# Loading one batch of queries transposed by DMA instead of transposing it on VectorE, in an attention-then-rational-MLP kernel

## The chip, the cores and the metric

The kernel runs on one core of a Trainium2 chip. The time is device microseconds of one execution, from start to end on that core. Three runs of the kernel before took 273.9, 274.3 and 274.56 us; the median is 274.3 us. All instruction times below come from one more execution, which the hardware profiler recorded.

## The reference

Two stages are chained. First an attention with polynomial sketches, for 4 batches, 4 heads, 1,088 positions and head width 32, all float32:

```python
def phi(x):                                  # 32 values -> 64 products
    a = einsum('rd,bhsd->bhsr', S1, x)       # 8 sketch values
    b = einsum('rd,bhsd->bhsr', S2, x)       # 8 sketch values
    return outer product of a and b, flattened
kv  = sum over s of phi(k)[f] * v[d]         # 64 x 32 per batch and head
z   = sum over s of phi(k)
x   = phi(q) @ kv / (phi(q) @ z + 1e-6)
```

The four heads side by side give 4,352 tokens (4 x 1,088) of width 128. Then a two-layer network of hidden width 2,048, with a rational function between the layers:

```python
h = x @ w_in
g = (a0 + a1*h + a2*h^2 + a3*h^3) / (1 + |b0|*|h| + |b1|*h^2 + 1e-6)
out = g @ w_out                              # 4352 x 128
```

## The kernel before

The whole program is written out by hand as one list of steps, `ORDER` (line 21). Each engine executes its own instructions strictly in the order in which that list produces them, so an instruction that waits holds back everything behind it on the same engine. The same holds for the queues on which DMAs are issued: SyncE (SP) issues nearly all of them, ScalarE (ACT) a few, each in its own program order.

**Keys and values.** Batch by batch, `load_k` and `load_v` (lines 116, 126) fetch them on SP's queue. There is one buffer for each (`k_sb`, `v_sb`). VectorE transposes the keys, TensorE makes the sketches, and the 64-value features times the values are summed on TensorE into a small table per batch (`kvz`).

**Queries.** They are worked off in 13 blocks: blocks 0 to 3 are batch 0, 4 to 6 batch 1, 7 to 9 batch 2, 10 to 12 batch 3; a block of batches 1 to 3 has 384, 384 or 320 positions. `load_q` (line 121) fetches a batch on SP's queue into the one buffer `q_sb`; the steps `lq:1`, `lq:2` and `lq:3` place these loads. In `q_sb` a partition holds a head and a group of positions, and VectorE turns 32x32 blocks (line 320, step `qt`) into `qT`, where a partition holds a head and one of the 32 components. Because of this blocking, column j*32+g of `qT` is position g*34+j; the store undoes that. TensorE makes the sketches of a block (line 401, step `qs`).

From block 3 on (class `Spread`) the sketches must be spread over 128 partitions, and this goes through DRAM, in `copies` (step `qc`): ScalarE copies the sketches out of PSUM (line 407), SP issues four small writes to DRAM (line 412), and, when these have landed, three reads that replicate the rows: one into `a_all` (line 415) and two into `b_all` (line 418). Then VectorE multiplies the two (line 424, step `qf`). TensorE multiplies the features with the table (line 360), VectorE divides, TensorE transposes back, and ScalarE writes the tokens into `xT` (line 390).

**Network.** The tokens are cut into 9 tiles (one of 256, eight of 512) and the work into 17 units of 128 x 4,096 values. For each, TensorE makes h (line 446), ScalarE brings it to SBUF as bf16 (line 452), VectorE forms the denominator (lines 475, 481, 486), ScalarE takes ln and exp(-ln) (lines 537, 541), VectorE multiplies (lines 545, 549, 560), and TensorE applies w_out (line 579). Finished tiles are stored by `store` (line 583): VectorE transposes the PSUM tile into `out_sb` (line 588; two buffers, from the pool `mid`), and four or eight DMAs write it out (line 596). The last tile's DMAs alternate between SP's and ACT's queue.

**Completion counters.** The framework attaches one of eight completion counters to every DMA, in turn, on all queues together. In the built program, a DMA whose counter was last used by another DMA waits on its own queue until that other DMA has landed, whether or not they share data.

The program also issues a few matmuls without use at the start (`turn`, line 166).

Of the kernel before, what the change touches and what calls it, by code (L numbers as in the profile page):

```python
# [11 lines left out]
FP = mybir.dt.float32  # L12
BF = mybir.dt.bfloat16
# [9 lines left out]
kf2:0 qc:0 kp0:0 qf:0 ks1:0 qs:1 kc1:0 kf1:0 qc:1 kp1:0 wo:1 qt:3 kp2:0 qf:1 qt:2 qs:3 kk:0 lq:1 wo:4 lv:1 qp:0 wo:0  # L23
qs:2 qd:0 qc:2 qi:0 qx:0 wo:5 qf:2 qb:0 qp:1 qk:0 qc:3 wo:3 h2:0 qd:1 qi:1 qx:1 kt0:1 h3:0 wo:2 e2:0 qt:5 qt:4 qp:2
kt1:1 e3:0 h1:0 pa1:0 u1:0 w1:0 h0:0 y1:0 qd:2 e1:0 qi:2 qx:2 qs:4 e0:0 qb:1 qb:2 qt:6 ks1:1 qk:1 u0:0 qk:2 ln1:0 w0:0
ks0:1 y0:0 h1:1 kc1:1 ex1:0 kf1:1 lk:2 h3:1 lq:2 e1:1 s1:0 kc0:1 h0:1 e3:1 kf0:1 pa0:0 m1:0 h2:1 qf:3 e0:1 x1:0 qp:3
qc:4 e2:1 kt0:2 h0:2 ln0:0 u1:1 kt1:2 h1:2 w1:1 e0:2 ex0:0 y1:1 ks0:2 h2:2 e1:2 s0:0 qd:3 ln0:1 h3:2 qi:3 m0:0 e2:2
lk:3 qx:3 kp1:1 x0:0 e3:2 ex0:1 u1:2 qb:3 lv:2 G0:0 pd0:1 qk:3 w1:2 ln1:1 G1:0 G2:0 qf:4 G3:0 kc0:2 kk:1 y1:2 ex1:1
G4:0 G5:0 kf0:2 qp:4 ln0:2 s0:1 qs:5 G0:1 qd:4 qc:5 qi:4 ex0:2 qt:7 G1:1 qx:4 m0:1 qb:4 ks1:2 qk:4 s1:1 pa1:1 h2:3
s0:2 kc1:2 m1:1 h3:3 e2:3 kf1:2 h1:3 e3:3 st:0 x1:1 ln1:2 qs:7 x0:1 h0:3 e1:3 kt1:3 m0:2 h2:4 e0:3 pd1:2 pa0:2 u1:3  # L30
h3:4 qt:9 w1:3 e2:4 G2:1 ex1:2 x0:2 h0:4 qf:5 e3:4 kp1:2 s1:2 pa0:3 y1:3 h1:4 qc:7 e0:4 m1:2 ln0:3 qp:5 kt0:3 e1:4
G3:1 x1:2 ex0:3 G4:1 m0:3 G5:1 u1:4 ks0:3 qd:5 ln1:3 qi:5 G0:2 w1:4 G1:2 pa1:3 qx:5 G2:2 y1:4 lv:3 qb:5 G3:2 qk:5
ex1:3 h0:5 m1:3 v0:3 kk:2 ln0:4 h2:5 s1:3 e0:5 qs:6 G4:2 qf:7 ex0:4 h1:5 x0:3 qt:8 qc:6 e2:5 s0:4 e1:5 h3:5 pd0:4
pa1:4 m0:4 h1:6 v1:3 e3:5 x0:4 G5:2 ln1:4 u1:5 h3:6 st:2 e1:6 w1:5 qp:7 ex1:4 x1:3 h0:6 e3:6 y1:5 qd:7 pa0:5 lq:3 G0:3
G2:3 qi:7 s1:4 h2:6 e0:6 m0:5 ln0:5 m1:4 qs:8 G3:3 e2:6 qf:6 G5:3 x1:4 ex0:5 G0:4 u1:6 G1:4 qc:8 ln1:5 qp:6 v0:5 qx:7
w1:6 qb:7 qd:6 G2:4 pa0:6 qi:6 G3:4 qx:6 y1:6 qb:6 qk:7 G4:4 qk:6 ex1:5 h3:7 m0:6 pa1:5 G5:4 qt:10 s1:5 h1:7 e3:7 st:4
h2:7 e1:7 m1:5 ln0:6 x0:5 h0:7 e2:7 x1:5 qs:9 e0:7 h3:8 qf:8 ex0:6 u1:7 h1:8 v0:6 qc:9 ln1:6 w1:7 ks1:3 s0:6 e1:8 G0:5
y1:7 kc1:3 qp:8 ex1:6 h2:8 pd1:6 kc0:3 e3:8 s1:6 ln0:7 h0:8 kf0:3 e2:8 m1:6 G2:5 ex0:7 G3:5 x0:6 G4:5 kf1:3 qd:8 e0:8
qs:10 G5:5 ln1:7 qi:8 u1:8 kp1:3 qx:8 pa0:7 w1:8 qb:8 G0:6 qf:9 qk:8 y1:8 qc:10 h3:9 ex1:7 s0:7 h2:9 e3:9 s1:7 ln0:8
h0:9 m0:7 e2:9 x1:6 G2:6 e0:9 h1:10 x0:7 ex0:8 pd1:7 h1:9 m1:7 pa0:8 s0:8 G3:6 e1:9 u1:9 G0:7 qt:11 ln1:8 qp:9 qt:12  # L40
u0:9 m0:8 h3:10 e1:10 w1:9 qd:9 ex1:8 qf:10 h2:10 x0:8 e3:10 G4:6 x1:7 e2:10 h0:10 y1:9 kk:3 pa0:9 w0:9 qp:10 qi:9
y0:9 e0:10 G1:7 qx:9 qd:10 ln0:9 qi:10 s1:8 qb:9 G5:6 u1:10 G2:7 qk:9 ex0:9 G3:7 qx:10 m1:8 qb:10 G4:7 qk:10 ln1:9
pd1:8 qs:11 h1:11 s0:9 qc:11 w1:10 ex1:9 h0:11 m0:9 e1:11 x1:8 G5:7 e0:11 h3:11 y1:10 pa1:9 G0:8 e3:11 s1:9 h2:11
ln0:10 x0:9 h0:12 m1:9 e2:11 pd0:10 ex0:10 h1:12 u1:11 x1:9 G1:8 ln1:10 G2:8 w1:11 G3:8 e0:12 s0:10 G0:9 e1:12 y1:11
G4:8 ex1:10 G5:8 G1:9 m0:10 ln0:11 G2:9 qf:11 h2:12 s1:10 ex0:11 x0:10 h3:12 pa1:10 m1:10 qs:12 G3:9 s0:11 e2:12 G4:9
pd0:11 qc:12 ln1:11 qp:11 m0:11 x1:10 G5:9 e3:12 G0:10 x0:11 qd:11 ex1:11 G1:10 qi:11 u1:12 G2:10 pa1:11 G3:10 qx:11
w1:12 qb:11 G4:10 qk:11 s1:11 pa0:12 h1:13 y1:12 h2:13 e1:13 m1:11 ln0:12 h3:13 st:6 x1:11 ex0:12 G5:10 qf:12 st:10
qp:12 e2:13 s0:12 e3:13 h0:13 st:8 ln1:12 m0:12 h2:14 u1:13 e0:13 x0:12 ex1:12 h3:14 u0:13 w1:13 e2:14 w0:13 G0:11
# [11 lines left out]
SPLIT_A = (0, 9, 13, 16)  # L60
QUARTER = (16,)
LX = 2
WIDE_S = (3, 5)
WIDE_M = (5,)
WIDE_X = (5, 14)
# [3 lines left out]
def kernel(  # L69
# [29 lines left out]
    consts = ctx.enter_context(tc.tile_pool(name="consts", bufs=1))  # L99
    big = ctx.enter_context(tc.tile_pool(name="big", bufs=1))  # L100
# [5 lines left out]
    mid = ctx.enter_context(tc.tile_pool(name="mid", bufs=2))  # L106
# [31 lines left out]
    for i, s_in in enumerate((S1, S2)):  # L138
        t = consts.tile([128, D], FP, name=f"s_raw{i}")
# [4 lines left out]
                      in_=bass.AP(tensor=k.tensor, offset=k.offset, ap=[[S * D // 32, 128], [W, NM], [1, 4 * D]]))  # L144
    nc.scalar.dma_start(out=k0[:, 0:km].rearrange("p (m x) -> p m x", m=NM - 1)[:, :, 4 * D:],
                        in_=k0_src[:, 0:km].rearrange("p (m x) -> p m x", m=NM - 1)[:, :, 4 * D:])
# [13 lines left out]
    w_out_sb_f = mid.tile([128, nf, d_model], FP, name="w_out_sb_f", tag="w", bufs=2)  # L160
    w_out_src = moe_w_out.rearrange("(fo fi) d -> fi fo d", fi=128)

    idle = consts.tile([128, 512], BF, name="idle")
    nc.vector.memset(idle, 0.0)

    def turn(i, cols=512):
        idle_ps = bank()
        for _ in range(TURNS[i]):
            nc.tensor.matmul(idle_ps[:, :cols], lhsT=idle[:, 0:128], rhs=idle[:, :cols], start=True, stop=True)

    mask = consts.tile([128, H], FP, name="mask")
    mask2 = consts.tile([128, 2], FP, name="mask2")
# [19 lines left out]
    for i in range(2):  # L192
        t = consts.tile([128, D], FP, name=f"sT{i}")
# [14 lines left out]
    for i in range(2):  # L208
        t = consts.tile([128, 2, R, R], FP, name=f"SAB{i}")
        s = sT[i][:, None, 0:R, None] if i == 0 else sT[i][:, None, None, 0:R]  # L210
# [10 lines left out]
    def bank():  # L221
        return att.tile([128, 512], FP, name="att_ps")
# [8 lines left out]
    class Keys:  # L231
# [80 lines left out]
    class Queries:  # L312
# [116 lines left out]
    TC = 512  # L429
# [112 lines left out]

    @skip(WIDE_S)
    def d_s(i, h, hh):
        nc.vector.tensor_mul(out=part_of(i, "s", h), in0=hh, in1=part_of(i, "r", h))  # L545
# [37 lines left out]
    def store(i):  # L583
        t0, tl, f0, per = units[i]
        if f0 + per < nf:
            return
        o = mid.tile([128, TC], FP, name="out_sb")
        nc.vector.transpose(out=o[:, :tl], in_=outs[t0][:, :tl])
        c = t0
        while c < t0 + tl:  # L590
            b = c // S
            ce = min(t0 + tl, (b + 1) * S)
            o_b = out[b * S:(b + 1) * S, :].rearrange("(g j) d -> g j d", g=32)
            j0, j1 = (c - b * S) // 32, (ce - b * S) // 32
            for e in range(d_model // 32):
                (nc.scalar if t0 + tl == n_tok and e % 2 else nc.sync).dma_start(
                    out=o_b[:, j0:j1, e * 32:(e + 1) * 32],
                    in_=o[e * 32:(e + 1) * 32, c - t0:ce - t0].rearrange("p (j d) -> p j d", d=32))
            c = ce
# [34 lines left out]
    def fetch_q(b):  # L634
        if b:
            return load_q(b)
        nc.sync.dma_start(out=q0[:, 512:S], in_=q0_src[:, 512:S])
# [71 lines left out]
```

## Time and profile before

| | us |
|---|---|
| median of three runs | 274.3 |
| the profiled execution, whole | 274.34 |
| its span in the trace | 272.6 |
| PE busy | 258.3 |
| DVE (VectorE) busy | 255.9 |
| ACT (ScalarE) busy | 250.0 |
| three transposes of batch 3's queries (line 320, at 116.4 and 152.6 us) | 1.5 |

The time around the span is 274.34 - 272.6 = 1.7 us. PE, DVE, ACT are the compute engines, SP is the engine whose queue issues DMAs; "SPq" in a line is that queue's own record. "L412" is line 412. In the lists of instructions the first number is the start in us from the start of the span, the second the duration in us; consecutive alike instructions are merged, and "x4" says how many. In the lists of waits the three numbers are the total wait in us, how many waits there were, and the longest.

TensorE's granted clock was 0.998 of full speed over the whole span.

### The profile page before, as it was taken

The page shows a single profiled execution, that of the slowest core. Times are in us where ns is not written, and L with a number is a line of the kernel's source. Part 1 is how long each engine was busy: PE and PEld are TensorE (multiplying, and loading weights), DVE is VectorE, ACT ScalarE, POOL GpSimd, SP SyncE. Part 2 cuts the span into 40 slices and gives each one's busy share as a digit, 9 for nine tenths or more (in the row PEclk, how much of TensorE's full clock was granted, in tenths as well). Part 3 has the DMA queues.
Part 4 walks back from the last instruction along what each step waited for, and adds up shares of the span by engine and source line. Part 5 has one row for each costly group of instructions (what it writes and reads, how often), then busy time and mean ns, then how long its engine had stood idle before and what let it go on. Part 6 is the DMA issues. An engine that isn't in the chain of part 4 may idle for free.

```text
span 272.6 us, 3564 instructions
## 1 busy us (share of the span) xinstructions
PE 258.3 (95%) x1318; PEld 135.4 (50%) x1318; DVE 255.9 (94%) x276; ACT 250.0 (92%) x224; POOL 2.9 (1%) x24
## 2 busy tenths in 40 slices
PE   7989999999999899999999999999999999989591
PEld 3778656963564354535454554434544443434230
DVE  2858999999999999999999999999999999999992
ACT  1377999998999999999999999999999999999980
POOL 4000000000000000000000000000000000000000
PEclk9999999999999999999999999999999999999999
DMA  6992607314025062222304000300126100020005
GB/s 166 294 336 80 204 14 173 111 55 95 2 84 129 14 140 77 73 71 39 96 6 117 11 1 6 120 6 0 23 88 96 20 0 0 0 41 1 0 0 77
DMA packets 30465, 19.53 MB, mean 72 GB/s; under 512 B 20337, under 2 KB 26609, under 8 KB 30449
## 3 DMA queue, kind: packets, MB, share of 16 engines
q1 hardware_dynamic: 28416, 18.87, 26.7%
q10 hardware_dynamic: 2032, 0.45, 0.9%
q8 instruction: 10, 0.16, 0.3%
q14 instruction: 7, 0.05, 0.1%
HBM read 16.16 MB, written 3.15 MB: 71 GB/s over the span
## 4 chain that ended last, share of the span: by engine, by line
PE 37%; ACT 28%; DVE 22%; issue 7%; DMA 2%; SPq 1%; DVEq 0%; ACTq 0%
PE h_ps L446 18%; PE att_ps L579 9%; ACT hh L452 8%; ACT ln L537 8%; ACT r L541 7%; ACT p L532 4%; DVE g L549 4%; DVE s L545 4%; DVE w L486 4%; PE att_ps L360 3%; DVE g L560 3%; DVE w L481 2%; DVE u L475 2%; DMA k_sb<-in_k_dram 2%; PE att_ps L297 1%
## 5 line engine op out<-in xcount | busy, mean ns | idle before, releaser
L446 PE MATMUL h_ps<-xT,w_in_sb 128*128 128x512 f32 (+1 forms) x288 | 125.4, 577 | 1.3 <-ACT hh L452 1.1
L446 PEld LDWEIGHTS h_ps<-xT,w_in_sb 128*128 128x128 f32 x288 | 52.2, 190 | 55.9 <-issue 40.5
L452 ACT CAST hh<-h_ps 128x1024 bf16<-128x1024 f32 x68 | 68.3, 1025 | 3.4 <-PE h_ps L446 2.9
L541 ACT ACTIVATE r<-ln 128x2048 bf16<-128x2048 f32 (+1 forms) x35 | 66.0, 1886 | 0.3
L537 ACT ACTIVATE ln<-w 128x2048 f32<-128x2048 bf16 (+1 forms) x35 | 66.0, 1885 | 0.2
L579 PEld LDWEIGHTS <-w_out 128*128 128x128 bf16 x412 | 39.9, 98 | 52.8 <-issue 18.7
L532 ACT ACTIVATE p<-hh,a_sb 128x2048 bf16<-128x2048 bf16 (+1 forms) x23 | 46.7, 2036 | 0.1
L545 DVE TENSOR_TENSOR s<-hh,r 128x2048 bf16<-128x2048 bf16 (+2 forms) x33 | 40.7, 1241 | 0.2
L486 DVE TENSOR_TENSOR w<-w,u 128x4096 bf16<-128x4096 bf16 (+2 forms) x22 | 39.5, 1795 | 0.1
L579 PE MATMUL att_ps<-g,w_out 128*128 128x512 bf16 (+1 forms) x144 | 34.9, 367 | 4.0 <-DVE g L560 3.8
L579 PE MATMUL att_ps<-r,w_out 128*128 128x512 bf16 (+1 forms) x144 | 34.5, 367 | 0.8 <-ACT r L541 0.8
L549 DVE TENSOR_TENSOR g<-hh,s 128x2048 bf16<-128x2048 bf16 (+1 forms) x30 | 35.1, 1172 | 0.0
L560 DVE TENSOR_TENSOR g<-g,p 128x2048 bf16<-128x2048 bf16 (+1 forms) x30 | 34.8, 1173 | 0.0
L579 PE MATMUL att_ps<-s,w_out 128*128 128x512 bf16 (+1 forms) x124 | 30.0, 365 | 0.0
L481 DVE TENSOR_SCALAR w<-u,b_abs 128x4096 bf16<-128x4096 bf16 (+2 forms) x22 | 23.8, 1090 | 0.1
L475 DVE TENSOR_SCALAR u<-hh 128x4096 uint16<-128x4096 uint16 (+2 forms) x22 | 21.3, 970 | 0.6 <-ACT hh L452 0.2
L360 PEld LDWEIGHTS att_ps<-kvz,q_pT 128*128 128x128 f32 x144 | 17.6, 191 | 5.0 <-DVE q_pT L424 1.1
L360 PE MATMUL att_ps<-kvz,q_pT 128*128 128x66 f32 x144 | 17.9, 273 | 0.9 <-DVE q_pT L352 0.5
L297 PEld LDWEIGHTS att_ps<-v_sb,k_p 128*64 128x64 f32 (+1 forms) x288 | 8.8, 138 | 2.6 <-issue 1.8
L527 DVE TENSOR_SCALAR p<-hh,a_sb 128x2048 bf16<-128x2048 bf16 x12 | 9.6, 804 | 0.0
L297 PE MATMUL att_ps<-v_sb,k_p 128*64 128x64 f32 (+1 forms) x288 | 9.5, 224 | 0.0
L424 DVE TENSOR_TENSOR q_pT<-a_all,b_all 128x768 f32<-128x768 f32 (+1 forms) x10 | 8.9, 895 | 0.0
(60 smaller groups left out, 134.9 us busy)
## 6 DMA issues: line engine op xcount, KB each, us to landing
a_all<-sk_d SPq DMA_DIRECT2D x6, 384.0 KB
b_all<-sk_d SPq DMA_DIRECT2D x12, 192.0 KB
v_sb<-in_v_dram SPq DMA_DIRECT2D x12, 144.0 KB
k_sb<-in_k_dram SPq DMA_DIRECT2D x3, 544.0 KB
q_sb<-in_q_dram SPq DMA_DIRECT2D x3, 544.0 KB
a_all<-sk_d SPq DMA_DIRECT2D x4, 320.0 KB
b_all<-sk_d SPq DMA_DIRECT2D x8, 160.0 KB
out_dram<-out_sb SPq DMA_DIRECT2D x18, 64.0 KB
```

Source lines behind the costliest of these rows:

```text
L360: nc.tensor.matmul(self.nd[:, o:o + 2 * KW], lhsT=self.q_p[:, c, x:x + 128], rhs=kvz[self.b % 2][:, c, :], start=True, stop=True)
L446: nc.tensor.matmul(t[:, x * tl:(x + 1) * tl], lhsT=w_in_sb[:, f * 128:(f + 1) * 128], rhs=xT[:, t0:t0 + tl], start=True, stop=True)
L452: nc.scalar.copy(out=live[i]["hh"][:, part * PW:(part + 1) * PW], in_=live[i]["h", part])
L481: nc.vector.tensor_scalar(out=t[:, c], in0=live[i]["u"][:, c], scalar1=ab1, scalar2=ab0, op0=AX.mult, op1=AX.add)
L486: nc.vector.tensor_mul(out=t[:, c], in0=t[:, c], in1=live[i]["u"][:, c])
L532: nc.scalar.activation(out=part_of(i, "p", h), in_=hh, func=ACT.Identity, scale=a3, bias=a2)
L537: nc.scalar.activation(out=t, in_=live[i]["w"][:, span(h)], func=ACT.Ln, bias=1.0 + 1e-6)
L541: nc.scalar.activation(out=part_of(i, "r", h), in_=live[i]["ln"], func=ACT.Exp, scale=-1.0)
L545: nc.vector.tensor_mul(out=part_of(i, "s", h), in0=hh, in1=part_of(i, "r", h))
L549: nc.vector.tensor_mul(out=part_of(i, "g", h), in0=hh, in1=part_of(i, "p" if horner(i, first(h)) else "s", h))
L560: nc.vector.tensor_mul(out=g, in0=g, in1=part_of(i, "s" if horner(i, first(h)) else "p", h))
L579: nc.tensor.matmul(outs[t0][:, :tl], lhsT=w_sb[y][:, f0 + x, :], rhs=part_of(i, key, h)[:, c:c + tl], start=done[0] == 0, stop=done[0] == ...
```

## The change

The queries of batch 3 are no longer loaded into `q_sb` by one DMA on SP's queue (it stood near 101 us). Four DMAs on ACT's queue, one per head, write them into a buffer of their own, `qT_sb`, already transposed: each reads a [1088, 32] matrix of float32 with its axes swapped. In the built program each of the four has 32 x 1,088 = 34,816 runs of one element (4 bytes). The step `lq:3` moves from line 34 of the list to right behind `lq:2`; in ACT's built order the four issues stand behind the first `r` (line 541) and ahead of the next copy of h (line 452). The three transposes of blocks 10 to 12 on VectorE fall away. Since the columns of `qT_sb` are positions in their natural order, the store uses another row order for batch 3.

To make room, the idle matmuls' tile shrinks from 512 to 128 columns (the matmuls read it four times over), and `out_sb` gets one buffer instead of two.

The built program numbers the completion counters 0 to 7. In the changed one the DMAs of this neighbourhood get them so: head 0 of the new load 6, keys of batch 2 counter 7, head 1 counter 0, queries of batch 2 counter 1, heads 2 and 3 counters 2 and 3. Then come the DMAs of block 4 and behind it: the four writes of its sketches 4, 5, 6, 7, its `a_all` 0, its two `b_all` 1 and 2, and the keys of batch 3 counter 3; the values of batch 2 and block 5's DMAs stand behind these on SP's queue.

```diff
 ORDER:  ... lk:2 h3:1 lq:2
+ lq:3
         e1:1 s1:0 kc0:1 ...          (line 26)
...
-pa1:4 m0:4 h1:6 v1:3 e3:5 x0:4 G5:2 ln1:4 u1:5 h3:6 st:2 e1:6 w1:5 qp:7 ex1:4 x1:3 h0:6 e3:6 y1:5 qd:7 pa0:5 lq:3 G0:3
+pa1:4 m0:4 h1:6 v1:3 e3:5 x0:4 G5:2 ln1:4 u1:5 h3:6 st:2 e1:6 w1:5 qp:7 ex1:4 x1:3 h0:6 e3:6 y1:5 qd:7 pa0:5 G0:3 G2:3
...
+NATURAL = (3,)
...
     def load_q(b):
+        if b in NATURAL:
+            t = big.tile([128, S], FP, name="qT_sb")
+            for h in range(H):
+                nc.scalar.dma_start(out=t[h * D:(h + 1) * D, :], in_=q[b, h].rearrange("s d -> d s"))
+            return t
...
-    idle = consts.tile([128, 512], BF, name="idle")
+    idle = consts.tile([128, 128], BF, name="idle")
...
         def transposes(self):
+            if self.b in NATURAL:
+                self.qT = self.q_sb[:, self.c0:self.c0 + self.n]
+                return
...
-        o = mid.tile([128, TC], FP, name="out_sb")
+        o = mid.tile([128, TC], FP, name="out_sb", bufs=1)
...
-            o_b = out[b * S:(b + 1) * S, :].rearrange("(g j) d -> g j d", g=32)
+            o_b = out[b * S:(b + 1) * S, :].rearrange("(j g) d -> g j d" if b in NATURAL else "(g j) d -> g j d", g=32)
```

More of the change, by code (lines that the diff above doesn't have):

```diff
@@ L25 @@
 kt1:1 e3:0 h1:0 pa1:0 u1:0 w1:0 h0:0 y1:0 qd:2 e1:0 qi:2 qx:2 qs:4 e0:0 qb:1 qb:2 qt:6 ks1:1 qk:1 u0:0 qk:2 ln1:0 w0:0
[L26 to L29, printed above, removed]
@@ L30 @@
-s0:2 kc1:2 m1:1 h3:3 e2:3 kf1:2 h1:3 e3:3 st:0 x1:1 ln1:2 qs:7 x0:1 h0:3 e1:3 kt1:3 m0:2 h2:4 e0:3 pd1:2 pa0:2 u1:3
-h3:4 qt:9 w1:3 e2:4 G2:1 ex1:2 x0:2 h0:4 qf:5 e3:4 kp1:2 s1:2 pa0:3 y1:3 h1:4 qc:7 e0:4 m1:2 ln0:3 qp:5 kt0:3 e1:4
-G3:1 x1:2 ex0:3 G4:1 m0:3 G5:1 u1:4 ks0:3 qd:5 ln1:3 qi:5 G0:2 w1:4 G1:2 pa1:3 qx:5 G2:2 y1:4 lv:3 qb:5 G3:2 qk:5
-ex1:3 h0:5 m1:3 v0:3 kk:2 ln0:4 h2:5 s1:3 e0:5 qs:6 G4:2 qf:7 ex0:4 h1:5 x0:3 qt:8 qc:6 e2:5 s0:4 e1:5 h3:5 pd0:4
-pa1:4 m0:4 h1:6 v1:3 e3:5 x0:4 G5:2 ln1:4 u1:5 h3:6 st:2 e1:6 w1:5 qp:7 ex1:4 x1:3 h0:6 e3:6 y1:5 qd:7 pa0:5 lq:3 G0:3
@@ L35 @@
[L35 to L44, printed above, removed]
@@ L45 @@
-G4:8 ex1:10 G5:8 G1:9 m0:10 ln0:11 G2:9 qf:11 h2:12 s1:10 ex0:11 x0:10 h3:12 pa1:10 m1:10 qs:12 G3:9 s0:11 e2:12 G4:9
+ks0:1 y0:0 h1:1 kc1:1 ex1:0 kf1:1 lk:2 h3:1 lq:2 lq:3 e1:1 s1:0 kc0:1 h0:1 e3:1 kf0:1 pa0:0 m1:0 h2:1 qf:3 e0:1 x1:0
+qp:3 qc:4 e2:1 kt0:2 h0:2 ln0:0 u1:1 kt1:2 h1:2 w1:1 e0:2 ex0:0 y1:1 ks0:2 h2:2 e1:2 s0:0 qd:3 ln0:1 h3:2 qi:3 m0:0
+e2:2 lk:3 qx:3 kp1:1 x0:0 e3:2 ex0:1 u1:2 qb:3 lv:2 G0:0 pd0:1 qk:3 w1:2 ln1:1 G1:0 G2:0 qf:4 G3:0 kc0:2 kk:1 y1:2
+ex1:1 G4:0 G5:0 kf0:2 qp:4 ln0:2 s0:1 qs:5 G0:1 qd:4 qc:5 qi:4 ex0:2 qt:7 G1:1 qx:4 m0:1 qb:4 ks1:2 qk:4 s1:1 pa1:1
@@ new lines @@
+h2:3 s0:2 kc1:2 m1:1 h3:3 e2:3 kf1:2 h1:3 e3:3 st:0 x1:1 ln1:2 qs:7 x0:1 h0:3 e1:3 kt1:3 m0:2 h2:4 e0:3 pd1:2 pa0:2
+u1:3 h3:4 qt:9 w1:3 e2:4 G2:1 ex1:2 x0:2 h0:4 qf:5 e3:4 kp1:2 s1:2 pa0:3 y1:3 h1:4 qc:7 e0:4 m1:2 ln0:3 qp:5 kt0:3
+e1:4 G3:1 x1:2 ex0:3 G4:1 m0:3 G5:1 u1:4 ks0:3 qd:5 ln1:3 qi:5 G0:2 w1:4 G1:2 pa1:3 qx:5 G2:2 y1:4 lv:3 qb:5 G3:2 qk:5
+ex1:3 h0:5 m1:3 v0:3 kk:2 ln0:4 h2:5 s1:3 e0:5 qs:6 G4:2 qf:7 ex0:4 h1:5 x0:3 qt:8 qc:6 e2:5 s0:4 e1:5 h3:5 pd0:4
+pa1:4 m0:4 h1:6 v1:3 e3:5 x0:4 G5:2 ln1:4 u1:5 h3:6 st:2 e1:6 w1:5 qp:7 ex1:4 x1:3 h0:6 e3:6 y1:5 qd:7 pa0:5 G0:3 G2:3
@@ new lines @@
+qi:7 s1:4 h2:6 e0:6 m0:5 ln0:5 m1:4 qs:8 G3:3 e2:6 qf:6 G5:3 x1:4 ex0:5 G0:4 u1:6 G1:4 qc:8 ln1:5 qp:6 v0:5 qx:7 w1:6
+qb:7 qd:6 G2:4 pa0:6 qi:6 G3:4 qx:6 y1:6 qb:6 qk:7 G4:4 qk:6 ex1:5 h3:7 m0:6 pa1:5 G5:4 qt:10 s1:5 h1:7 e3:7 st:4 h2:7
+e1:7 m1:5 ln0:6 x0:5 h0:7 e2:7 x1:5 qs:9 e0:7 h3:8 qf:8 ex0:6 u1:7 h1:8 v0:6 qc:9 ln1:6 w1:7 ks1:3 s0:6 e1:8 G0:5 y1:7
+kc1:3 qp:8 ex1:6 h2:8 pd1:6 kc0:3 e3:8 s1:6 ln0:7 h0:8 kf0:3 e2:8 m1:6 G2:5 ex0:7 G3:5 x0:6 G4:5 kf1:3 qd:8 e0:8 qs:10
+G5:5 ln1:7 qi:8 u1:8 kp1:3 qx:8 pa0:7 w1:8 qb:8 G0:6 qf:9 qk:8 y1:8 qc:10 h3:9 ex1:7 s0:7 h2:9 e3:9 s1:7 ln0:8 h0:9
@@ new lines @@
+m0:7 e2:9 x1:6 G2:6 e0:9 h1:10 x0:7 ex0:8 pd1:7 h1:9 m1:7 pa0:8 s0:8 G3:6 e1:9 u1:9 G0:7 qt:11 ln1:8 qp:9 qt:12 u0:9
+m0:8 h3:10 e1:10 w1:9 qd:9 ex1:8 qf:10 h2:10 x0:8 e3:10 G4:6 x1:7 e2:10 h0:10 y1:9 kk:3 pa0:9 w0:9 qp:10 qi:9 y0:9
+e0:10 G1:7 qx:9 qd:10 ln0:9 qi:10 s1:8 qb:9 G5:6 u1:10 G2:7 qk:9 ex0:9 G3:7 qx:10 m1:8 qb:10 G4:7 qk:10 ln1:9 pd1:8
+qs:11 h1:11 s0:9 qc:11 w1:10 ex1:9 h0:11 m0:9 e1:11 x1:8 G5:7 e0:11 h3:11 y1:10 pa1:9 G0:8 e3:11 s1:9 h2:11 ln0:10
+x0:9 h0:12 m1:9 e2:11 pd0:10 ex0:10 h1:12 u1:11 x1:9 G1:8 ln1:10 G2:8 w1:11 G3:8 e0:12 s0:10 G0:9 e1:12 y1:11 G4:8
@@ L46 @@
+ex1:10 G5:8 G1:9 m0:10 ln0:11 G2:9 qf:11 h2:12 s1:10 ex0:11 x0:10 h3:12 pa1:10 m1:10 qs:12 G3:9 s0:11 e2:12 G4:9
 pd0:11 qc:12 ln1:11 qp:11 m0:11 x1:10 G5:9 e3:12 G0:10 x0:11 qd:11 ex1:11 G1:10 qi:11 u1:12 G2:10 pa1:11 G3:10 qx:11
@@ L168, in turn @@
         for _ in range(TURNS[i]):
-            nc.tensor.matmul(idle_ps[:, :cols], lhsT=idle[:, 0:128], rhs=idle[:, :cols], start=True, stop=True)
+            nc.tensor.matmul(idle_ps[:, :cols].rearrange("p (x y) -> p x y", y=128), lhsT=idle,
+                             rhs=idle[:, None, :].broadcast_to([128, cols // 128, 128]), start=True, stop=True)
     mask = consts.tile([128, H], FP, name="mask")
```

## The prediction

> **What bounds the kernel now.** I read the page first, busy times and slices:
>
> ```profile
> PE 258.3 (95%) x1318; PEld 135.4 (50%) x1318; DVE 255.9 (94%) x276; ACT 250.0 (92%) x224; POOL 2.9 (1%) x24
> DVE  2858999999999999999999999999999999999992
> DMA  6992607314025062222304000300126100020005
> ```
>
> From about 25 us on three engines are full at once. A microsecond that VectorE (DVE) loses in the middle has nowhere to go but the end; one that it is spared is worth at most itself. The DMA engines are mostly idle.
>
> Then the waits of SP's own queue, because the change puts a long transfer among its neighbours:
>
> ```profile
> SPq L412 <- ACT sk_sb L407: 98.1, 10, 22.7
> SPq L412 <- DMA q_sb<-in_q_dram: 1.9, 1, 1.9
> SPq L131 <- DMA k_sb<-in_k_dram: 1.7, 2, 1.2
> ```
>
> The first is idleness. The second carries my forecast: a write of block 3's sketches (L412) waited 1.9 us for a load of queries, with which it shares no data, only the completion counter. So counters do hold up SP's queue.
>
> Last the order of time, of SP and of DVE around block 4 and of the stores:
>
> ```profile
> 37.59 1.72 SPq L412 DMA_DIRECT2D sk_d<-sk_sb  x4
> 40.59 0.55 SPq L415 DMA_DIRECT2D a_all<-sk_d  x1
> 41.19 1.23 SPq L418 DMA_DIRECT2D b_all<-sk_d  x2
> 42.52 0.39 SPq L118 DMA_DIRECT2D k_sb<-in_k_dram  x1
> ```
>
> ```profile
> 50.75 0.95 DVE L424 TENSOR_TENSOR q_pT<-a_all,b_all 128x768 f32<-128x768 f32 x1
> 51.62 2.29 DVE L486 TENSOR_TENSOR w<-w,u 128x4096 bf16<-128x4096 bf16 x1
> ...
> 71.78 0.95 DVE L424 TENSOR_TENSOR q_pT<-a_all,b_all 128x768 f32<-128x768 f32 x1
> ```
>
> ```profile
> 203.62 0.70 DVE L588 STREAM_TRANSPOSE out_sb<-att_ps 128x512 f32<-128x512 f32 x1
> ...
> 206.17 0.72 DVE L588 STREAM_TRANSPOSE out_sb<-att_ps 128x512 f32<-128x512 f32 x1
> ...
> 207.92 0.70 DVE L588 STREAM_TRANSPOSE out_sb<-att_ps 128x512 f32<-128x512 f32 x1
> ```
>
> DVE needs block 4's `a_all` and `b_all` at 50.75 us and block 5's at 71.78; both are there in time now, and DVE runs without a gap. Three stores follow each other within 5 us.
>
> **What it saves.** Three transposes, 0.57 us and a pair of 0.96: **-1.5 us**. The old load on SP (issued at 100.9) was hidden; its going is worth nothing.
>
> **The new load.** 34,816 runs of 4 bytes per head over 16 DMA engines are 2,176 per engine and head, 8,704 in all. The trace has no such load, so the price r of one run on one engine is bounded. The packet records of before show: the 16-byte packets of L153's load, from ACT's queue too, took 9 ns each and, where eight followed each other undisturbed, started 5.9 ns apart; 4-byte packets (the counters' updates) took 9 ns; 128-byte packets took 13.6 ns, and in the burst of stores at 99 us, held back by its issues, came 17 ns apart per engine. Ends: 5.9 and 17 ns. I take r = 9 ns, what the packets nearest in size took; 5.9 was seen only for eight in a row.
>
> The four issues stand behind the `r` that ends at 32.3 us on ACT. Issues in this trace take 0.3 to 0.7 us for 32 rows as for 1,024, so I charge ACT 2 us; what follows hides that. Transfers begin near 33.0 (0.6 us from issue to first packet, as for the store at 63.57) and the heads go one after the other, so head n (0 to 3) lands at 33.0 + 2.176 r (n+1). At 9 ns: 52.6, 72.2, 91.8 and 111.3 us. The data itself is wanted only after 116 us: as a transfer, it would be hidden.
>
> **The waits that it adds.** By the built program block 4's third sketch write shares a counter with head 0, its `a_all` with head 1, its second `b_all` with head 2, and the keys of batch 3, next on SP's queue, with head 3. Behind that stand the values of batch 2 and all of block 5. So SP stops at 38 us.
>
> - Block 4: the last `b_all` is issued when head 2 lands, at 91.8, plus 0.6 issue and 2.6 to land (estimated from block 5's, issued by 61.1, whose packets end near 63.7): 95.0 instead of by 50.75. DVE stands still for 44.3 us.
> - Block 5: SP goes on at 111.3 (head 3): key load 0.4, value loads 1.8, the sketch chain as before from 56.35 to 61.08 (4.7), landing 2.6: 120.8, instead of by 71.78. That is 49.0 us late, 4.7 more than the first wait. The larger counts, for the waits overlap: **+49.0 us**.
>
> TensorE and ACT can go on only until they need block 4's tokens (TensorE's L360 at 54.0 us), so nothing is won back. The later blocks find their counters free.
>
> **One buffer of `out_sb`.** A store's transpose must wait until the DMAs of the store before have landed. Four issues take 1.97 us; landing I take as 1.2 us after the last issue (sketch writes: issues end at 58.06, L415 starts at 59.24). The store at 206.17 then waits until 204.34 + 1.97 + 1.2 = 207.5 (1.3 us); the next, due at 209.2, until 211.4 (2.2 us). The last store waits for the one before it: 266.04 + 1.97 + 1.2 = 269.2 instead of 267.26 (1.9 us), and nothing is behind it. DVE has no gap there: **+5.4 us**, bounded by 0 (gaps open that cover it) and 8 (landing a microsecond slower).
>
> The idle tile and the order of the stored rows cost nothing: same matmuls, same 128-byte rows.
>
> **Sum**, against the profiled execution's 274.34 us (the median of the runs is 274.3): 274.34 - 1.5 + 49.0 + 5.4 = **327 us**. With r the first wait is 6.53 r - 14.6, the second 8.70 r - 29.3; the larger rules: 24 us at 5.9 ns (302 us), 89 at 13.6 (367 us), 119 at 17 (397 us).
>
> [...]
>
> **The rivals.**
>
> 1. Short runs, r below 7 ns, the spacing of the 16-byte packets. For it: nothing else competes while SP stands. Against: eight packets are no steady state, and a run here is an own read from DRAM. 290 to 311 us, 302 at 5.9 ns. [...]
> 2. Long runs, r above 11.5 ns: 128-byte packets took 13.6, and scattered 4-byte reads may be no better. 367 us at 13.6 ns.
> 3. ACT itself is held. If its queue takes no further load before an earlier one is through, the fourth issue waits for head 2, and ACT's next copy, due at 32.2 us, comes at 91.8: 59.6 us, within which SP's waits then lie. 274.34 - 1.5 + 59.6 + 5.4 = 338 us. For it: ACT's queue is in order. Against: issue times here do not depend on the row count.
> 4. Not slower: the load is through before SP comes round. For that head 2 must land by 50.75 - 3.2 = 47.5 us, three heads in 14.5 us, r at most 2.2 ns; this is the point that decides. Then 274.34 - 1.5 = 273 us, if the stores' waits are covered too, 278 if not. For it: runs from one matrix might be fetched together. Against: 2.2 ns is well under half of the smallest spacing in the trace.
>
> **How the numbers follow.** Forecast (r from 7 to 11.5 ns) 0.45, rival 1 0.23, rival 2 0.17, rival 3 0.09, rival 4 0.06 (0.03 faster, 0.02 no change, 0.01 slower at 278). The range, 294 to 372 us, leaves out rival 4, the quickest part of rival 1 and the slow half of rival 2 beyond 14.1 ns: some 0.17 in all. Faster by over 0.2% (about what a measurement of this kernel can tell from no change) 0.03, within 0.2% 0.02, slower 0.95.
>
> **What would show it.** SP's waits should name the transposing load ahead of L412, L415 or L418 and the key load, tens of us each; DVE should have one gap of some 44 us ahead of the second L424 (line 434 in the changed kernel) and a short one ahead of the third; some 139,000 packets of 4 bytes should stand on ACT's DMA queue, from 33 to about 111 us. The three later `out_sb` transposes should wait for DMAs, 1 to 2 us each. If DVE runs on past 51 us, the counters do not hold SP, and the forecast is wrong in its main term; if the gap is there but of another length, r is. If ACT is idle from 34 us on while DVE still works, it is rival 3.

## The result, and the profile after

The changed kernel takes 350.94 us (median of four runs, 350.55 to 352.98) where the kernel before took 274.34 beside it: a ratio of 1.281 [1.2757, 1.2862]. The profiled execution took 350.55 us, its span is 348.7.

The page of the changed kernel: VectorE's busy time, the slices of VectorE and of TensorE's granted clock, and ACT's DMA queue (q10: packets, MB, share of 16 engines).

```profile
PE 263.8 (76%) x1318; PEld 138.1 (40%) x1318; DVE 255.1 (73%) x273; ACT 251.1 (72%) x224; POOL 2.9 (1%) x24
DVE  4677000000189398999999999999999779999991
PEclk9999555555599969999999999999999999999896
q10 hardware_dynamic: 141360, 1.00, 40.9%
```

VectorE's and ScalarE's busy times are as before, TensorE's is 5.5 us longer; in six slices of 8.7 us none of the three does anything. ACT's order of time around them (start, duration; "idle before" in brackets):

```profile
30.12 0.64 ACTq L126 DMA_DIRECT2D qT_sb<-in_q_dram  x1
30.13 1.94 ACT L551 ACTIVATE r<-ln 128x2048 bf16<-128x2048 f32 x1
30.80 62.37 ACTq L126 DMA_DIRECT2D qT_sb<-in_q_dram  x3
93.21 1.01 ACT L462 CAST hh<-h_ps 128x1024 bf16<-128x1024 f32 x1 [61.15 <-issue]
```

The first of the four issues took 0.64 us. The other three took 21.72, 20.25 and 20.33 us, one after the other, and ACT's next copy of h, behind them in ACT's order, waited 61.15 us ("issue": for nothing else that the profile shows). The three waited for the load ahead, but not until it had landed: they ended at 52.52, 72.80 and 93.17 us, and by the completion counters heads 0 to 2 had landed at 55.24, 75.63 and 96.13. VectorE's two waits that follow, in order of time (`k_p`, the features of the keys, needs ACT's copy `b_sk`), with the first of them in the kernel before:

```profile
33.47 1.22 DVE L268 TENSOR_TENSOR k_p<-att_ps,b_sk 128x1024 f32<-128x1024 f32 x1
```

```profile
94.43 1.23 DVE L275 TENSOR_TENSOR k_p<-att_ps,b_sk 128x1024 f32<-128x1024 f32 x1 [61.10 <-ACT b_sk L270]
...
118.96 0.96 DVE L434 TENSOR_TENSOR q_pT<-a_all,b_all 128x768 f32<-128x768 f32 x1 [5.68 <-DMA b_all<-sk_d]
```

The first is ACT's. The second is block 4's sketches: the last `b_all` was issued by 107.6 us and by its completion counter had landed at 118.8, 11.2 us later. In the kernel before the same one took 5.8 us and block 5's 4.6. Head 3 was being loaded at that time. The sketch writes ahead were slow beside it too: from their first issue to `a_all` it took 6.7 us instead of 3.0. SP's own waits, to set against the forecast:

```profile
SPq L422 <- ACT sk_sb L417: 156.0, 10, 69.6
...
SPq L119 <- DMA qT_sb<-in_q_dram: 13.7, 1, 13.7
```

SP waited 69.6 us for ACT's copy of the sketches (L417, before L407). The only wait for the new load is the key load's, 13.7 us; the keys are wanted later, and nothing is lost by it. Last the stores, in VectorE's waits:

```profile
DVE out_sb L598 <- DMA out_dram<-out_sb: 7.3, 3, 3.0
```

From these rows and those of before the 76 us can be added up, by how much later VectorE reaches the same instruction:

| VectorE reaches | before | after | later by |
|---|---|---|---|
| the first `k_p` behind the issues (L268, now L275) | 33.47 | 94.43 | 61.0 |
| block 4's `q_pT` (L424, now L434) | 50.75 | 118.96 | 68.2 |
| block 5's | 71.78 | 141.54 | 69.8 |
| first of the three stores (L588, now L598) | 203.62 | 273.56 | 69.9 |
| third of them | 207.92 | 282.21 | 74.3 |
| last store | 267.26 | 343.69 | 76.4 |

So: 61.0 ACT held at its issues; 7.2 block 4, most of it the slow `b_all`; 1.6 up to block 5; 4.4 and 2.1 at the stores. Between block 5 and the first store the three transposes fall away, and the shift does not shrink (69.8, 69.9).

### The profile page after: what moved, and what is told of

Same layout as the page of the kernel before. It is cut to its first block, busy times and chain, and to the rows that moved or that the text cites. A ratio compares the mean times of both kernels' runs of the same rounds, so it can differ in the third digit from the quotient of the medians.

```text
span 348.7 us, 3570 instructions
## 1 busy us (share of the span) xinstructions
PE 263.8 (76%) x1318; PEld 138.1 (40%) x1318; DVE 255.1 (73%) x273; ACT 251.1 (72%) x224; POOL 2.9 (1%) x24
## 3 DMA queue, kind: packets, MB, share of 16 engines
q10 hardware_dynamic: 141360, 1.00, 40.9%
## 4 chain that ended last, share of the span: by engine, by line
ACT 21%; PE 20%; DVE 19%; ACTq 18%; issue 8%; DMA 8%; SPq 3%; DVEq 0%
ACTq L126 18%; PE h_ps L456 12%; ACT ln L547 6%; ACT r L551 6%; ACT hh L462 5%; DVE g L559 4%; PE att_ps L589 4%; DMA b_all<-sk_d 3%; DVE s L555 3%; ACT p L542 3%; DVE w L496 3%; DMA out_dram<-out_sb 2%; DVE g L570 2%; PE att_ps L370 2%; SPq L606 2%
## 5 line engine op out<-in xcount | busy, mean ns | idle before, releaser
L456 PE MATMUL h_ps<-xT,w_in_sb 128*128 128x512 f32 (+1 forms) x288 | 126.9, 582 | 62.4 <-ACT hh L462 62.2
L462 ACT CAST hh<-h_ps 128x1024 bf16<-128x1024 f32 x68 | 68.2, 1022 | 66.5 <-issue 61.1
L456 PEld LDWEIGHTS h_ps<-xT,w_in_sb 128*128 128x128 f32 x288 | 53.1, 192 | 117.4 <-ACT hh L462 71.3
L589 PEld LDWEIGHTS <-w_out 128*128 128x128 bf16 x412 | 40.7, 100 | 55.8 <-issue 23.0
L275 DVE TENSOR_TENSOR k_p<-att_ps,b_sk 128x1280 f32<-128x1280 f32 (+1 forms) x6 | 8.1, 1353 | 61.3 <-ACT b_sk L270 61.3
L589 PE MATMUL att_ps<-g,w_out 128*128 128x512 bf16 (+1 forms) x144 | 35.8, 374 | 3.6 <-DVE g L570 3.6
L589 PE MATMUL att_ps<-r,w_out 128*128 128x512 bf16 (+1 forms) x144 | 36.1, 380 | 2.4 <-ACT r L551 1.6
L589 PE MATMUL att_ps<-s,w_out 128*128 128x512 bf16 (+1 forms) x124 | 30.8, 373 | 0.0
L485 DVE TENSOR_SCALAR u<-hh 128x4096 uint16<-128x4096 uint16 (+2 forms) x22 | 21.4, 976 | 3.5 <-ACT hh L462 3.4
L434 DVE TENSOR_TENSOR q_pT<-a_all,b_all 128x768 f32<-128x768 f32 (+1 forms) x10 | 9.0, 898 | 5.7 <-DMA b_all<-sk_d 5.7
L598 DVE STREAM_TRANSPOSE out_sb<-att_ps 128x512 f32<-128x512 f32 (+1 forms) x9 | 6.1, 682 | 7.3 <-DMA out_dram<-out_sb 7.3
```

Of the source, the lines that this page charges most:

```text
L456: nc.tensor.matmul(t[:, x * tl:(x + 1) * tl], lhsT=w_in_sb[:, f * 128:(f + 1) * 128], rhs=xT[:, t0:t0 + tl], start=True, stop=True)
L462: nc.scalar.copy(out=live[i]["hh"][:, part * PW:(part + 1) * PW], in_=live[i]["h", part])
L589: nc.tensor.matmul(outs[t0][:, :tl], lhsT=w_sb[y][:, f0 + x, :], rhs=part_of(i, key, h)[:, c:c + tl], start=done[0] == 0, stop=done[0] == ...
```

## The experiments

In the expectations **theory A** says: an issue on a queue is held until the element-wise load that was issued before it on that queue is through, 20 us a head; ACT's instructions behind the held issues wait with them. **S** says that the stores' waits go straight to the end. The rivals stand in each text.

### One buffer of out_sb alone

In the kernel before, one line:

```diff
-        o = mid.tile([128, TC], FP, name="out_sb")
+        o = mid.tile([128, TC], FP, name="out_sb", bufs=1)
```

> The kernel before with one buffer of out_sb, nothing else changed. Theory S (each store's transpose waits until the DMAs of the store before have landed, and VectorE or the end pays it): the changed kernel shows waits of 1.8, 2.5 and 3.0 us ahead of three of these transposes, so about 274.3 + 7 = 281 us (my step before said +5.4). Rival (gaps elsewhere take up the first two, only the last store's wait counts): about 277 us. If the waits belong to the loads, not to the buffer: 274 us.

280.56 us, ratio 1.0218 [1.0201, 1.0236]: 6.1 us, close to the 7 that S adds. Two of VectorE's waits stand in one line; the first of the three, 1.73 us at 208.74 us, the profile puts down to a matmul (L360) instead:

```profile
DVE out_sb L588 <- DMA out_dram<-out_sb: 5.4, 2, 3.0
```

### One head by elements, last or first

In the changed kernel three heads are read as contiguous rows (their data is then not transposed), and only head 3, or only head 0, by elements:

```diff
-                nc.scalar.dma_start(out=t[h * D:(h + 1) * D, :], in_=q[b, h].rearrange("s d -> d s"))
+                src = q[b, h].rearrange("s d -> d s") if h == 3 else q[b, h].rearrange("(p x) d -> p (x d)", p=D)
+                nc.scalar.dma_start(out=t[h * D:(h + 1) * D, :], in_=src)
```

> The changed kernel, but heads 0 to 2 of batch 3 come as contiguous rows of 4,352 bytes, untransposed (their values are in the wrong places); only head 3, the last of the four issues on ACT, is read element by element. Counters and order stay. Theory A (an issue on ACT is held while an earlier element-by-element load is under way): no issue stands behind the long load, ACT is not held, all four issues take under 1 us each; what is left is the stores' 7 us, the three transposes' -1.5 and some slowing of block 4's spread-back by the load beside it: 280 to 285 us. Theory C (the counters hold SP): only the key load waits for head 3, until about 53 us, and nobody needs it then: the same 280 to 285. Rival H (the long load holds ACT itself, wherever it stands): one issue of 20 us, about 300 us.

> As the run with the last head alone, but now head 0, the first of the four issues, is read element by element and heads 1 to 3 come as contiguous rows, untransposed. Theory A: the second issue on ACT is held until head 0 is through, 20 to 22 us, as in the changed kernel; 274.3 + 20 + 7 - 1.5, about 300 us. Theory C (ACT not held, the third write of block 4's sketches waits for head 0's counter until about 51 us): block 4's features 8 us late at most, about 285 to 288 us. Rival H: an issue of 20 us too, but the first one, not the second.

Head 3 alone, issued last: 288.07 us, ratio 1.0494 [1.0471, 1.0518]. The four issues took 0.35 to 0.66 us, and ACT was not held. SP's wait for it and VectorE's wait at block 4:

```profile
SPq L119 <- DMA qT_sb<-in_q_dram: 16.7, 1, 16.7
```

```profile
57.54 0.96 DVE L435 TENSOR_TENSOR q_pT<-a_all,b_all 128x768 f32<-128x768 f32 x1 [6.76 <-DMA b_all<-sk_d]
```

The key load waited 16.7 us and cost next to nothing: block 5's `q_pT` follows block 4's after 21.4 us (78.94), against 21.0 before, and no wait stands ahead of it. What cost is 6.8 us at block 4, whose `b_all` was issued by 46.0 and came at 57.5 beside the load. That is above the 280 to 285 us expected, by this slowing.

Head 0 alone, issued first: 304.57 us, ratio 1.1096 [1.1073, 1.1118], some 5 us above the 300 expected. The issue behind it took 21.46 us though it is a load of rows, and ACT's copy waited:

```profile
53.36 1.01 ACT L463 CAST hh<-h_ps 128x1024 bf16<-128x1024 f32 x1 [21.19 <-issue]
```

The load is the same, only its place among the four differs. So what matters is an issue behind it on the queue, as A says, and not the load's own issue.

### Eight halves instead of four heads

```diff
-                nc.scalar.dma_start(out=t[h * D:(h + 1) * D, :], in_=q[b, h].rearrange("s d -> d s"))
+                for x in range(0, S, S // 2):
+                    nc.scalar.dma_start(out=t[h * D:(h + 1) * D, x:x + S // 2],
+                                        in_=q[b, h, x:x + S // 2].rearrange("s d -> d s"))
```

> The changed kernel with each head's load cut into two halves of 544 positions: eight DMAs instead of four, the same 139,264 runs. Theory A (an issue waits until the load before it is nearly through): ACT is free again when the seventh of eight is through, 7/8 instead of 3/4 of the whole 82 us, so held 71 us instead of 61, and the time is about 10 us longer than the changed kernel's: 358 to 362 us. Rival B (the queue has room for a fixed number of runs, about one head's): held 61 us as before, 350 us. If issues are dear in themselves: more than 365 us.

354.67 us, ratio 1.2921 [1.2881, 1.296]. By A seven of eight pieces are waited for: 7/8 of four times 20.4 is 71.4 us. ACT's wait:

```profile
ACT hh L464 <- issue: 71.8, 1, 71.8
```

The hold came out as worked out, and a fixed room for runs in the queue (rival B, 61 us) is out. The total grew by 4, not by 10, and misses the 358 to 362 us expected: block 4's `b_all` no longer ran beside the load, and VectorE's 5.7 us there shrank to 0.7. That is 5 of the 7 us that are missing.

### The same four loads on SP's queue, and late on ACT's

`nc.sync` in place of `nc.scalar`; and, by itself, the step `lq:3` back at its old place in the list (near 101 us), still on ACT's queue.

> The changed kernel with its four loads issued on SP's queue instead of ACT's. Theory A, for any queue: SP's issues are held, 20 to 22 us for each of the second to fourth, and block 4's sketch writes, next on SP, come after 91 us; its features then some 62 us late; ACT and DVE run on to about 50 us before they stand: 338 to 348 us. Rival (it is ACT's own matter): SP's issues take under 1 us, and block 4 waits only by its counters, until head 2 has landed near 92 us and a few us more: 322 to 332 us.

> The changed kernel with the step lq:3 back at its old place (line 34 of the list, about 100 us), still four loads on ACT. Theory A: ACT is held 61 us there just the same, and the time is about the changed kernel's, 338 to 350 us: less block 4's 7 us of slow spread-back, more some 5 us because the last head lands only 82 us after the first issue. Rival (the hold comes from the early place, with the loads of batch 2 still on their way): held clearly shorter than 55 us.

On SP's queue: 357.33 us in a single run. SP's order of time:

```profile
28.23 65.76 SPq L126 DMA_DIRECT2D qT_sb<-in_q_dram  x4
94.08 21.75 SPq L422 DMA_DIRECT2D sk_d<-sk_sb  x4
```

ACT is free now, and SP is held, also at the small writes behind the fourth load: 21.75 us for four writes that take 1.7 us elsewhere. So it is not ACT's own matter, and what is issued behind the load need not be long. The time is above the 338 to 348 us expected for that reason: the fourth head is waited for as well.

Late on ACT's queue: 345.7 us, ratio 1.26 [1.2563, 1.2636], as expected. ACT's wait is there too, at 162 us:

```profile
ACT hh L462 <- issue: 57.6, 1, 57.6
```

The place in the kernel changes little.

### On GpSimd's queue

Twelve pieces (a head by 384, 384 or 320 positions) on GpSimd's queue, started near 28 us, and again started later:

```diff
-                nc.scalar.dma_start(out=t[h * D:(h + 1) * D, :], in_=q[b, h].rearrange("s d -> d s"))
+            for x, y in ((0, 384), (384, 768), (768, S)):
+                for h in range(H):
+                    nc.gpsimd.dma_start(out=t[h * D:(h + 1) * D, x:y], in_=q[b, h, x:y].rearrange("s d -> d s"))
```

> [...] Theory A (the 61 us come from ACT being held at its issues, not from the data being late or the counters): ACT runs on; left are block 4's spread-back beside the load (7 us, as with the last head alone), the stores' 6 us, -1.5 us, and perhaps a few us at blocks 5 and 7: 285 to 295 us. [...]

> As on GpSimd's queue, but starting near 50 us (behind block 3's tokens), past block 4's spread-back. Theory A with contention as the rest of the cost: block 4's 7 us are gone, block 5's features have 8 us to spare and block 7's 7, so 0 to 4 us there; the stores' 6 us and the -1.5 us stay: 279 to 283 us. Rival (each block's spread-back beside the load loses more than it has to spare): 285 us or more.

Early: 295.77 us, ratio 1.078 [1.0739, 1.0821], just above the range. ACT and SP are free, and block 4 is reached at 50.69 us as before. Late: 314.35, ratio 1.1457 [1.1325, 1.159], a miss; the data itself came too late for TensorE, which the waits show:

```profile
PE att_ps L413 <- DMA qT_sb<-in_q_dram: 26.9, 2, 26.2
```

GpSimd needs 3.2 to 4.4 us to issue a piece and pauses between two (11 pauses, 126.5 us in all in the early run, 116.8 in the late one, the longest 16.6 us), so the last piece was issued at 195 us in one and at 213 us in the other. Of the early one's 21.5 us the stores' waits are 7.3 and late data 2.2; VectorE's busy time is 264.6 us there, 9.5 above the changed kernel's, but only 256.3 in the late one. Its order of time, with GpSimd's beside it, shows where this goes:

```profile
78.98 3.72 POOL L128 DMA_DIRECT2D qT_sb<-in_q_dram  x1 [12.93 <-issue]
```

```profile
80.29 3.43 DVE L487 TENSOR_SCALAR u<-hh 128x4096 uint16<-128x4096 uint16 x1
```

Such an instruction takes 1.2 us elsewhere; this one began during GpSimd's issue (78.98 to 82.70) and ended 1.0 us after it. Five TENSOR_SCALAR instructions of the early run began so; each ended 0.5 to 1.0 us after the issue, 0.7 to 2.8 us late, 10.4 us in all. In the late run two began so and lost 2.0 us together. Instructions of other kinds that began during an issue took their usual time. With the 7.3 and 2.2 that makes 19.9 of the 21.5 us.

### The four heads spaced out

Head by head on ACT's queue, 34 to 38 us apart. `load_q` only makes the list of transfers, and steps `lp:0` to `lp:3` stand at four places of `ORDER`:

```diff
+            parts[b] = [(t[h * D:(h + 1) * D, x:y], q[b, h, x:y].rearrange("s d -> d s"))
+                        for h, x, y in [(0, 0, 1088), (1, 0, 1088), (2, 0, 1088), (3, 0, 1088)]]
...
+        elif name == "lp":
+            o, i_ = parts[3][i]
+            nc.scalar.dma_start(out=o, in_=i_)
```

> The changed kernel with the same four loads on ACT's queue, not back to back but some 20 to 35 us apart in ACT's own work (near 32, 56, 90 and 114 us). Theory A (an issue is held only until the element-wise load before it on its queue is through, some 20 us): no issue is held, each costs ACT under 1 us, and the 61 us are gone; what is left is 6 to 7 us at the stores, 7 us at block 4's small DMAs if they meet a load, less 1.5, and 0 to 10 us for other small DMAs that meet one: 283 to 296 us. Rival (every element-wise load after the first costs its issuing engine its 20 us, whenever it is issued): ACT held three times for 20 us, about 350 us.

313.86 us, ratio 1.1437 [1.1417, 1.1458]. The issues, in the list of the tile's instructions (ns, least/median/most), and SP's waits for the load:

```profile
L688 ACTq DMA_DIRECT2D qT_sb<-in_q_dram x4: 587/610/656, 30.6 to 138.3; - x4
```

```profile
SPq L608 <- DMA qT_sb<-in_q_dram: 33.2, 2, 18.5
SPq L424 <- DMA qT_sb<-in_q_dram: 17.8, 1, 17.8
SPq L430 <- DMA qT_sb<-in_q_dram: 12.5, 1, 12.5
```

No issue is held, so A's main statement stands and its rival falls. But the time is 18 us above A's range, and the reason is the one that the forecast named: with ACT free, SP waits for the load through shared counters. Ahead of `b_all` (L430) it stood 12.5 us; SP's order of time at block 4 (before: 40.59 and 41.19):

```profile
44.53 0.55 SPq L427 DMA_DIRECT2D a_all<-sk_d  x1
57.56 1.23 SPq L430 DMA_DIRECT2D b_all<-sk_d  x2
```

VectorE waits for `b_all` four times, 31.3 us in all (12.7, 4.4, 7.3, 7.0), and at the stores 7.3; the span grew by 39.5.

### The same, with head 0 on another counter

One step moved, so that the first `b_all` of block 4 no longer shares head 0's counter:

```diff
-lq:2 lq:3 lp:0 e1:1 s1:0 kc0:1 h0:1 e3:1 kf0:1 pa0:0 m1:0 h2:1 qf:3
+lq:2 lq:3 e1:1 s1:0 kc0:1 h0:1 e3:1 kf0:1 pa0:0 m1:0 h2:1 lp:0 qf:3
```

> The kernel with the four spaced heads, with one step moved: head 0 is issued some 4 us later on ACT (near 34.6 instead of 30.6 us), behind the loads of keys and queries of batch 2 in the built program, so that its completion counter is next used by the key load of batch 3 and no longer by the first b_all of block 4. If it was the counter that held SP at b_all for 12.5 us with spaced heads (L430 waiting for qT_sb): that wait goes, b_all is issued near 46 us, and what is left of VectorE's 12.7 us ahead of block 4 is the slow landing beside the load, 5 to 8 us as with one head by elements; SP waits for qT_sb at the key load instead, which costs nothing: 313.9 less 5 to 8, so 306 to 309 us. Rival (all of it is contention, and the counter only coincides): head 0 runs 4 us later, VectorE's wait stays at 12 us or grows to 17, and the time at 313 to 318 us.

313.13 us (309.99 to 313.85), ratio 1.1368 [1.1302, 1.1435]: the total is hardly lower, above the 306 to 309 us expected and where the rival had put it. SP's order of time at block 4, SP's waits, and VectorE's at blocks 4 and 7:

```profile
44.55 0.55 SPq L427 DMA_DIRECT2D a_all<-sk_d  x1
45.16 1.23 SPq L430 DMA_DIRECT2D b_all<-sk_d  x2
```

```profile
SPq L424 <- DMA qT_sb<-in_q_dram: 22.0, 1, 22.0
SPq L119 <- DMA qT_sb<-in_q_dram: 15.2, 1, 15.2
```

```profile
57.59 0.96 DVE L436 TENSOR_TENSOR q_pT<-a_all,b_all 128x768 f32<-128x768 f32 x1 [6.50 <-DMA b_all<-sk_d]
...
108.85 0.96 DVE L436 TENSOR_TENSOR q_pT<-a_all,b_all 128x768 f32<-128x768 f32 x1 [10.12 <-DMA b_all<-sk_d]
```

At block 4, though, it went as expected and not as the rival has it: `b_all` is issued at 45.2 instead of 57.6, SP's wait stands at the key load, and VectorE's wait fell from 12.7 to 6.5 us, which is the slow landing that head 3 alone had shown (6.8). Nearly all of the 6.2 us were given back at block 7, the next but one in the list. Its sketch writes were held by head 1's counter until 96.1 us (22.0 us of waiting; 17.8 and 97.4 with the other place of head 0), and VectorE, there earlier, waited 10.1 us instead of 4.4. So the counter is shown as the cause of that wait; in the total the next held write decides.

### No transposes at all

In the kernel before, batch 3's three transposes are left out (its sketches come from untransposed data):

```diff
+            if self.b == 3:
+                self.qT = self.q_sb[:, self.c0:self.c0 + self.n]
+                return
```

> The kernel before, with the three transposes of batch 3's queries left out (the sketches of batch 3 are made from the untransposed data, so this part of the computation is changed); the load stays one DMA on SP's queue. It measures the most that the change can give. If VectorE's time goes straight to the end, as the prediction has it: 1.5 us less, about 272.8 us, ratio 0.9945. Rival, the three are hidden because PE or ACT ends later there: within 0.5 us of the kernel before, ratio 0.998 to 1.002.

274.45 us, ratio 1.0003 [0.9993, 1.0013]: they are worth nothing, and the rival holds. Block 8's `q_pT` came 0.2 us early (122.83) and block 9's 0.1 late (140.44); batch 3's first came 0.3 early (155.61) and its second 0.1 late (186.75). VectorE's waits in that stretch show most of the reason:

```profile
124.30 1.23 DVE L478 TENSOR_SCALAR u<-hh 128x4096 uint16<-128x4096 uint16 x1 [0.52 <-ACT hh L455]
153.14 0.69 DVE L478 TENSOR_SCALAR u<-hh 128x2048 uint16<-128x2048 uint16 x1 [0.41 <-ACT hh L455]
163.08 0.23 DVE L378 RECIPROCAL rec<-den 128x12 f32<-128x12 f32 x1 [0.66 <-ACT den L374]
```

In the kernel before the first of these is 0.23 us, the second is not there, and the third is 0.32: together 1.0 of the 1.5 us is now spent in waiting for ACT, which is due at nearly the same time. Where the rest goes the waits do not show.

### Twelve small pieces, two buffers again

Twelve pieces on ACT's queue, each behind another `r`, from 52 to 184 us; room for the second `out_sb` comes from a lone `x_tok` buffer and a borrowed tile:

```diff
+                        for h, x, y in [(0, 0, 384), (1, 0, 384), (2, 0, 384), (3, 0, 384), (0, 384, 768), ...
-            self.x = tmp.tile([128, 3, 128], FP, name="x_tok")
+            self.x = tmp.tile([128, 3, 128], FP, name="x_tok", bufs=1)
-        o = mid.tile([128, TC], FP, name="out_sb", bufs=1)
+        o = mid.tile([128, TC], FP, name="out_sb")
```

> The changed kernel with the load cut into 12 pieces (a head by 384, 384 or 320 positions, 6 to 7 us each at 9.4 ns per run and engine), one behind each of 12 activations of ACT's own work between about 52 and 178 us, and out_sb with two buffers again (the room comes from one x_tok buffer instead of two and from a borrowed tile for the idle matmuls). Theory A: no issue is held, no store waits; the 12 issues cost ACT 0.5 us each at most, the transposes save 1.5, and what small DMAs lose beside the pieces decides: 273 to 280 us; it can be faster than the kernel before only if they lose less than about 1.5 us. Rival (each piece costs ACT its length, or the lone x_tok buffer makes VectorE wait): 283 us or more, with ACT held at the issues in the trace, or with waits at x_tok.

281.96 us, ratio 1.027 [1.0242, 1.0299]: the least of all ways of loading by elements, and still slower, 2 us above A's range. Nine issues took 0.3 us; three came before the piece ahead of them was through and took 1.4 to 3.6. ACT's queue, and SP's order of time:

```profile
118.97 0.32 ACTq L689 DMA_DIRECT2D qT_sb<-in_q_dram  x1
...
126.12 3.60 ACTq L689 DMA_DIRECT2D qT_sb<-in_q_dram  x1
```

```profile
120.13 11.63 SPq L609 DMA_DIRECT2D out_dram<-out_sb  x8
```

A piece 7.2 us behind another one still waited: the three waits ended 9.9 to 10.8 us after the issue of the piece ahead (10,240 or 12,288 runs), beside other transfers, and not the 6 to 7 assumed. The eight stores took 11.6 us, 6.2 of them a wait for a piece's counter (4.9 us in the kernel before), and the sketch chain behind them made VectorE wait 3.4 us. Most of the loss lies there: block 8's `q_pT` was 1.9 us late and block 9's 7.5. Some 0.7 us had been lost before the first piece, where VectorE waited 1.2 us at 27.7 us for the lone `x_tok` buffer.

## Why the prediction was wrong, and where it was right

The direction and the range held; the mechanism that carried the 327 us did not. That 351 lies in the range is luck: it reaches so far for long runs (rival 2), and the runs were as short as forecast.

**The step that failed** is "Issues in this trace take 0.3 to 0.7 us for 32 rows as for 1,024, so I charge ACT 2 us". The four issues took 63.0 us, of which ACT lost 61. The rows of before reach 1,024 runs per DMA; these have 34,816, and they had no other such load ahead of them. That was an extrapolation of 34 times, and it was also the whole argument against rival 3, which had the mechanism and 0.09. Its sum, 338 us, lacks 13: hold 61.0 for 59.6, block 4's slow landing 7.2 and 1.6 more to block 5, which nobody had, stores 6.5 for 5.4, and transposes worth nothing instead of 1.5. The signs named for the forecast stayed away: SP waited for the load at the key load alone, and VectorE's gap stood at `k_p` from 33.3 us on, not at block 4. The sign for rival 3, ACT idle while VectorE still works, did not show either, for VectorE needed ACT's next copy about a microsecond later.

**The counters (+49.0).** In the changed kernel they cost nothing: block 4's writes wait for ACT's copy of the sketches, and that comes behind the fourth issue, when heads 0 to 2 are as good as through. Only head 3's counter was left, at the key load. But the mechanism was real: with ACT free, SP stood 12.5 us at `b_all` by head 0's counter, and one moved step took the wait away. The forecast described the kernel that it would have been without the hold.

**The price of a run.** The chosen 9 ns was right. The packet records show 4-byte packets from 31.7 to 120 us, 3,400 in 2 us on 16 engines, 9.4 ns per run and engine; a head took 20.4 us. ACT's queue (q10) has 139,328 packets more than before (141,360 against 2,032): the 139,264 runs, and 64 updates of counters. The range's lower end, 294 us, belongs by the forecast's own sum to about 4.7 ns per run. No run shows such a price: four heads took 88 us, 9.4 ns per run and engine.

**The landing of block 4 (charged 2.6 us)** was 11.2, with the last head still loading. The prediction had this `b_all` go out as head 2 lands, so beside head 3, but took a landing without such a neighbour. And that one was misread: the last packet of block 5's `b_all` ends at 64.8 us, not 63.7, and its counter is complete at 65.7, which makes 4.6 us. The first packet behind the store at 63.57 came after 0.9 us, not 0.6. Both together would have raised the forecast by some 2 us.

**One buffer (+5.4):** 6.1 us by itself, 6.5 in the changed kernel. The waits are 1.8, 2.5 and 3.0 for 1.3, 2.2 and 1.9; in the kernel before the DMAs of the store at 203.62 had landed 1.5 us after their last issue, not 1.2.

**The transposes (-1.5):** 0, between -0.2 and +0.4 us by the interval. That three engines at 92 to 95% leave VectorE no cover was right for a loss, and wrong for a gain: ACT was due just behind. So the change had nothing to win, wherever its load is put.

**TensorE's clock** fell to 0.50 at 36.0 us, 2.8 us after TensorE had stopped (33.2), and returned at 97.4, 3.1 us after it had begun again at 94.3 (the 5s in the profile). TensorE's busy time rose by 5.5 us; how much of it reached the end was not separated.

## What to carry to other kernels

Before a transfer is moved to another queue, count its runs and look at what that engine does next: here a load of four times 34,816 runs of 4 bytes was hidden as data (its packets ended near 120 us, TensorE first read it at 206.5), and still held the issues behind it on its queue, 20 to 22 us each, and with them ACT for 61 us. Where issue times come from small DMAs, do not carry them to one with 34 times the runs. And first measure what the removed work is worth by leaving it out: here one such run would have told that there was nothing to gain.

## What the runs showed of the hardware

- An issue behind an element-wise load of a whole head was held until near the end of that load, on ACT's queue (19.6 to 21.7 us a head) and on SP's (19.6 to 25.0), also when it was a load of rows (21.46 us) or a small write of sketches (four writes 21.75 us instead of 1.7). In the changed kernel the holds ended 2.7 to 3.0 us before the load ahead had landed. The first issue took 0.6 to 0.7 us in each of these runs: the load's own issue was short, and the next one on its queue paid. The other queue went on (four writes in 1.7 us on SP while head 3 loaded, and with spaced heads while head 0 did). What holds the issue, no run here shows.
- In the changed kernel 4-byte runs cost 9.4 ns per engine in steady flow, and the 557 KB took 88 us. Where small transfers ran beside it, a head took longer: head 3's packets 26.5 us (93.5 to 120.0) instead of 20.4, and spaced heads 27.9 to 29.4 us from issue to landing, against 25.1 for head 0 of the changed kernel. Block 4's last read landed after 11.2 us instead of 5.8.
- GpSimd's queue issued a piece about every 15 us (12 from 29 to 195 us). A TENSOR_SCALAR instruction of VectorE that began during such an issue ended only 0.5 to 1.0 us after it (seven cases in two runs, up to 2.8 us late).
